# A new schedule for the attention and expert layers: fills costed at half rate first, measured durations, a new priority table

## The chip, the cores and the metric

The kernel runs on one core of one Trainium2 chip. The metric is device time in microseconds (us) of one execution. Every measured run computes the whole reference.

## The reference

Chunked attention over q, k and v of shape (4, 8, 768, 64): each chunk of 32 queries sees its own keys, 16 before, 8 after and 8 memory rows. Its output, as 3072 tokens of 512, goes through eight experts, weighted by a routing matrix that eight rounds of row and column scaling make.

```python
for c in range(nc):
    scores = scale * np.matmul(q_c, k_full.transpose(0, 1, 3, 2))
    scores = scores - np.max(scores, axis=-1, keepdims=True)
    a = np.exp(scores)
    a = a / (np.sum(a, axis=-1, keepdims=True) + 1e-09)
    out[:, :, c_start:c_end] = np.matmul(a, v_full)
...
logits = x @ w_gate
P = np.exp(logits - logits.max())
for _ in range(8):
    P /= P.sum(1, keepdims=True) + 1e-09
    P /= P.sum(0, keepdims=True) + 1e-09
    P *= N / E
for e in range(E):
    h = np.maximum(x @ w1[e], 0.0)
    ye = h @ w2[e]
    out += P[:, e:e + 1] * ye
```

## The kernel before, in words

The tokens come in 24 attention blocks of 128 queries; four blocks make a unit of 512 tokens, and there are six units. Each of the eight experts works through the six units. A product of two f32 numbers is done as three f16 products (a high and a low part of each), and the products of experts 1 to 7 go through a seven-product scheme on 2 by 2 blocks instead of eight products.

The start is what this case is about. For block n the names in the profile are these: `tq` and `tk` are TensorE (PE) transposes of q and k, `tx` that of the keys that other blocks share (`kx`), `sp` the scores, `ta` the transpose of the weights after the exponential, `xp` the product with the values (`v_pair` for blocks 0 and 1, `x_room` for some of the later ones), `gram_v` and `gram_w` PE products whose trace bounds the size of a tile, `norm_x` and `norm_w` the sums over partitions that turn such bounds into scales. `xg` is the attention output and `x` its f16 halves. `pp` is the first expert's hidden layer, `yp` its output. Later `px`, `py`, `pz` and `yx`, `yy`, `yz` do this for the other experts. `w1f` and `w2f` are the weights as they come from memory, four tiles of 512 KB each for expert 0; a tile of q or k is 256 KB, the values of one block 448 KB in pieces of up to 56 KB.

Nothing in the program text sets the order. Each step is a task with an engine, a cost in us and a priority, and `Plan.run` puts the tasks in order as if it ran them: each engine takes next the ready task of least priority value, and the instructions are issued in that order. The priority is a due time plus an entry of the table `MOVED`, by task number. In that plan a load through SyncE (SP) or GpSimd (POOL) lands after a fixed latency and a term for its bytes, at most eight are on their way at a time on either, and a task can start when those it waits for have ended. Where the plan sees PE with nothing to do for over 0.4 us, `pad` issues fills: matmuls of 256 columns whose result nobody reads (`warm` in the profile), so many that they take 0.8 of the gap at 0.11 us each. On the chip each engine runs its queue in order and waits by semaphores; a fill runs whether the gap is there or not.

The identity matrix is written by POOL; the fills read it as bf16. `v_pair` gets the eight memory rows of its batch from POOL: two small loads (`mem_v`, line 1110), and then two copies that spread them over the chunks (line 1128), which wait for the loads.

Of the kernel before, what the change touches and what calls it, by code (L numbers as in the profile page):

```python
# [120 lines left out]
class Plan:  # L121
# [73 lines left out]
    def run(self):  # L195
        clock = {e: 0.7 for e in self.ENGINES}
        waiting = {e: [] for e in self.ENGINES}
# [7 lines left out]
        while left:  # L205
# [50 lines left out]
            else:  # L256
                clock[t.eng] = t.end = at + t.cost
# [9 lines left out]
            lag = 0.0 if t.dma else 0.2 if t.eng == "PE" else 0.12  # L267
# [15 lines left out]
def tile_chunked_attn_sinkhorn_moe(  # L283
# [85 lines left out]
    idle = ident.bitcast(BF16)  # L369
# [4 lines left out]
    pscale = misc.tile([P, E, NT], F32, name="pscale")  # L374
# [273 lines left out]
    def cut(e, fp, which, st, ld, prio):  # L648
# [37 lines left out]
        for op in ops:  # L686
            sums.append(add("POOL", 0.95, tt(*op), [ld] + sums[-1:], prio - 5, [st, ws]))
# [27 lines left out]
        else:  # L715
            pieces = [(slice(2, 3), slice(0, 1), (0.5, 0.65)), (slice(4, 7), slice(1, 4), (0.9, 1.1))]
# [25 lines left out]
    def squares(total, src, deps, prio, bufs):  # L742
# [6 lines left out]
        return add("ACT", 1.2, go, deps, prio, bufs)  # L749

    def norm_scale(c, r, u, shift, name, deps, prio, slow=False):
# [24 lines left out]
        if slow:  # L776
# [12 lines left out]
            0.3,  # L789
# [14 lines left out]
    def gram(total, parts, name, deps, prio, bufs, m=P):  # L804
# [8 lines left out]
        t = add("PE", 0.5, go, deps, prio - FIRM, bufs, takes=g)  # L813
# [5 lines left out]
        return add("DVE", 0.5, trace, [t], prio, frees=g)  # L819
# [6 lines left out]
    def norm_of(fp, which, st, ld, on, prio):  # L826
# [19 lines left out]
        return c, add("DVE", 1.31, go, [ld], prio, [st])  # L846
# [38 lines left out]
    def plain1(fp, st, ld, prio):  # L885
# [9 lines left out]
                (0.6, 0.72),  # L895
# [76 lines left out]
    def load_extra(u):  # L972
# [47 lines left out]
        def part(r, loads, at, tx, takes):  # L1020
            t = add("PE", 0.6, lambda: turn(r), loads, at, [kx, kxT], takes=takes)
# [67 lines left out]
    def load_values(n):  # L1089
# [68 lines left out]
        if n < BU:  # L1158

            if n > 1:  # L1160

                vmem[slot] = b
                lv = [add("POOL", 2.0, take_m, vs[0][1], at, [vt, vs[0][0]])]
# [16 lines left out]
        else:  # L1180
            lv = []
            if BU <= n < EARLY:
                vmem[slot] = b
                lv = [add("POOL", 2.0, take_m, vs[0][1], VALUES[-1], [vt, vs[0][0]])]
# [29 lines left out]
        elif n in BY_DVE:  # L1214
# [5 lines left out]
            vfound.append(add("DVE", 1.31, most, lv, at, [vt]))  # L1220
# [11 lines left out]
    def transposed(n):  # L1232
# [35 lines left out]
        t = add("PE", 0.5, go_q, [lq], at, [qt, qT], takes=tq)  # L1268
# [1355 lines left out]
```

## Time and profile before

| | us |
|---|---|
| median of three runs | 1907.76 (1907.01 to 1907.77) |
| profiled execution | 1908.04 |
| its span, first to last instruction | 1905.9 |
| PE busy in it | 1890.7 |
| VectorE (DVE) busy | 1452.3 |
| ScalarE (ACT) busy | 1046.9 |
| POOL busy | 537.6 |

PE is busy for 99% of the span, but busy counts the 103 fills too, all in the first 50 us, and the end of a matmul is modelled: a gap of some 0.15 us behind a group does not show. What can be saved without changing the arithmetic is the time in which PE does fills or waits.

### The profile page before, as it was taken

To read this page: it belongs to the slowest core of one execution; us is meant where nothing else is said; L and a number is where in the kernel's file an instruction comes from. 1 tells how busy PE (TensorE), PEld (TensorE's weight loads), DVE (VectorE), ACT (ScalarE), POOL (GpSimd) and SP (SyncE) were. 2 spreads that over 40 slices of the span, in tenths; PEclk is the share of its full clock that TensorE was granted. 3 is DMA by queue.
4 is the path that set the end of the run, shared out by engine and by line. 5 is a ranking of instruction groups with operands and counts; after the bars stand their busy time and mean duration, and the time that the engine had idled before them with its cause. 6 is when DMAs were issued, how large, how long until landed. Compare 5 with 4: busy or idle time off the path is not lost.

```text
span 1905.9 us, 47378 instructions
## 1 busy us (share of the span) xinstructions
PE 1890.7 (99%) x19598; PEld 1629.7 (86%) x19598; DVE 1452.3 (76%) x2447; ACT 1046.9 (55%) x2047; POOL 537.6 (28%) x599
## 2 busy tenths in 40 slices
PE   8999999999999999999999999999999999999999
PEld 7677676788888888888888888888888888888888
DVE  6777669887689866888669876898678885786565
ACT  5776665655565555456456544655555563564453
POOL 3331212413134212522224131442124231332112
PEclk9999999999999999999999999999999999999999
DMA  9977744533324441364234432245313732322321
GB/s 200 206 179 219 180 156 144 174 138 112 122 87 153 167 149 46 94 230 149 84 99 164 148 128 106 89 161 184 122 46 118 247 106 103 93 84 87 125 84 67
DMA packets 207128, 254.76 MB, mean 134 GB/s; under 512 B 106112, under 2 KB 140016, under 8 KB 202560
## 3 DMA queue, kind: packets, MB, share of 16 engines
q1 hardware_dynamic: 204960, 249.63, 41.1%
q0 software_dynamic: 1952, 2.11, 0.6%
q8 instruction: 153, 2.51, 0.6%
q14 instruction: 63, 0.52, 0.1%
HBM read 187.83 MB, written 63.44 MB: 132 GB/s over the span
## 4 chain that ended last, share of the span: by engine, by line
PE 92%; DMA 3%; DVE 2%; SPq 1%; issue 1%; ACT 0%; POOL 0%; ACTq 0%; DVEq 0%; POOLq 0%
PE px L1825 25%; PE yx L1825 22%; PE pz L1825 12%; PE yz L1825 11%; PE py L1825 6%; PE yy L1825 6%; PE yp L2422 5%; PE xp L1375 1%; DMA q<-in_q_dram 1%; PE sp L1308 1%; SPq L1141 1%; DVE ss L1994 0%; DMA v_pair<-in_v_dram 0%; PE tq L1245 0%; PE ta L1365 0%
## 5 line engine op out<-in xcount | busy, mean ns | idle before, releaser
L1825 PEld LDWEIGHTS <-w 128*128 128x128 f16 x7896 | 771.4, 98 | 94.9 <-issue 4.1
L1825 PEld LDWEIGHTS <-h 128*128 128x128 f16 x7056 | 690.4, 98 | 81.5 <-issue 1.4
L1825 PE MATMUL px<-x,w 128*128 128x256 f16 x4512 | 548.5, 273 | 1.5 <-DVE c L1895 1.3
L2159 POOL TENSOR_TENSOR acc<-acc,y 128x256 f32<-128x256 f32 x252 | 263.5, 1052 | 875.5 <-ACT y L2134 862.6
L1825 PE MATMUL yx<-w,h 128*128 128x256 f16 x4032 | 468.0, 273 | 0.7 <-DVE acc L2169 0.5
L1885 ACT ACTIVATE q<-px 128x256 f32<-128x256 f32 x376 | 143.1, 382 | 286.6 <-PE px L1825 282.4
L1825 PE MATMUL pz<-x,w 128*128 128x256 f16 x2256 | 278.4, 273 | 0.0
L1825 PE MATMUL yz<-w,h 128*128 128x256 f16 x2016 | 233.8, 273 | 0.0
L2054 DVE TENSOR_TENSOR h<-ss,h 128x1024 f16<-128x1024 f32 x168 | 217.2, 1295 | 3.6 <-ACT h L2030 3.6
L2005 ACT ACTIVATE h<-c 128x768 f16<-128x768 f32 x168 | 141.0, 840 | 114.3 <-DVE c L1895 114.3
L2030 ACT CAST h<-ss 128x1024 f16<-128x1024 f32 x168 | 174.4, 1041 | 39.7 <-DVE ss L1994 39.7
L1994 DVE SCALAR_TENSOR_TENSOR ss<-c,ss 128x256 f32<-128x256 f32 x336 | 176.4, 525 | 8.5
L2038 DVE SCALAR_TENSOR_TENSOR h<-c,h 128x768 f16<-128x768 f32 x168 | 170.1, 1016 | 9.2 <-ACT h L2005 9.2
L1895 DVE SCALAR_TENSOR_TENSOR c<-px,q 128x256 f32<-128x256 f32 x188 | 77.8, 421 | 94.3 <-PE px L1825 89.0
L2134 ACT ACTIVATE y<-yx,pscale 128x256 f32<-128x256 f32 x168 | 79.8, 475 | 119.6 <-PE yx L1825 115.2
L1825 PE MATMUL py<-x,w 128*128 128x256 f16 x1128 | 139.1, 273 | 1.3 <-DVE c L1895 0.8
L2422 PE MATMUL yp<-w,h 128*128 128x512 f16 x576 | 130.9, 379 | 0.0
L1994 DVE SCALAR_TENSOR_TENSOR ss<-c,h 128x512 f32<-128x512 f32 x168 | 125.7, 748 | 1.9 <-ACT h L1982 1.9
L1895 DVE SCALAR_TENSOR_TENSOR c<-py,q 128x256 f32<-128x256 f32 x188 | 78.0, 421 | 62.0 <-PE py L1825 59.6
L1825 PE MATMUL yy<-w,h 128*128 128x256 f16 x1008 | 116.9, 273 | 0.0
L2422 PEld LDWEIGHTS <-h 128*128 128x128 f16 x576 | 55.3, 99 | 60.1 <-issue 0.2
L1895 DVE SCALAR_TENSOR_TENSOR c<-pz,q 128x256 f32<-128x256 f32 x188 | 78.2, 422 | 25.4 <-PE pz L1825 23.7
(193 smaller groups left out, 1767.2 us busy)
## 6 DMA issues: line engine op xcount, KB each, us to landing
x<-xkeep SPq DMA_DIRECT2D x28, 1792.0 KB
akeep<-acc SPq DMA_DIRECT2D x168, 256.0 KB
acc<-akeep SPq DMA_DIRECT2D x168, 256.0 KB
w1f<-in_moe_w_dram SPq DMA_DIRECT2D x36, 512.0 KB
w2f<-in_moe_w_dram SPq DMA_DIRECT2D x32, 512.0 KB
w1fm<-in_moe_w_dram SPq DMA_DIRECT2D x28, 512.0 KB
w2fm<-in_moe_w_dram SPq DMA_DIRECT2D x28, 512.0 KB
xkeep<-x SPq DMA_DIRECT2D x6, 1792.0 KB
```

Source lines behind the costliest of these rows:

```text
L1141: queue.dma_start(vt.t[p0 + r : p0 + r + m, c, :, 0:D], v[b, par::2, t : t + m].rearrange("h t d -> t h d"),)
L1825: nc.tensor.matmul(dst.t, a, b, start=(not more and n == 0), stop=(n == end), skip_group_check=more,)
L1885: lambda: nc.scalar.activation(t.t, src.t, AF.Copy, scale=down),
L1895: lambda: nc.vector.scalar_tensor_tensor(c.t[:, o], src.t, down, q.t, op0=ALU.mult, op1=ALU.add),
L1994: lambda: nc.vector.scalar_tensor_tensor(dst(), src(), 0.0, other(), op0=ALU.max, op1=op),
L2005: lambda: nc.scalar.activation(h.t[:, 0, 0:3], c.t, AF.Relu),
L2030: lambda: nc.scalar.copy(h.t[:, 0, 3:7], ss.t),
L2038: lambda: nc.vector.scalar_tensor_tensor(h.t[:, 1, 0:3].rearrange("p a n -> p (a n)"), c.t.rearrange("p a n -> p (a n)"), 0.0, h.t[:, 0, 0 ...
L2054: lambda: spare.tensor_tensor(h.t[:, 1, 3:7], ss.t, h.t[:, 0, 3:7], op=ALU.subtract),
L2134: (lambda: nc.scalar.activation(t.t, src.t, AF.Copy, scale=f))
L2159: lambda: nc.gpsimd.tensor_tensor(acc.t[:, cols], acc.t[:, cols], q.t, op=ALU.add),
L2422: nc.tensor.matmul(py.t, hf.t[:, hl, where[fh], o : o + P], room(fp, WIDE * wl + DM * fh, WIDE * wl + DM * (fh + 1)), start=(fp == 0 and i ...
```

## The change

The arithmetic and its instructions stay; the order of the instructions, the number of the fills and what they read change. Five parts:

- `pad` counts fills at 0.22 us each up to 6.9 us (`COLD`) and at 0.11 us beyond, starts no earlier than 1.1 us, and keeps the bank taken until the gap's end. PE tasks that start before 6.9 us count double.
- The fills read `pscale`, a tile that DVE clears as its first instruction; before they read the identity.
- An engine is free for the next task a little before the end of the last one (`OVER`), the latency from ACT, DVE and POOL to another engine goes from 0.12 to 0.07 us, and POOL starts at 1.6 us.
- Some thirty task costs are set to other values, PE's mostly lower, DVE's mostly higher.
- The table `MOVED` has other entries.

```diff
 MOVED = {
-    0: -85.9, 1: 16.9, 3: -259.1, 8: 9, 10: 220.9, 14: -3.9, 15: -12.2, 21: -4.5, 27: 32.3, 28:
+    3: 39.9, 8: 8.4, 11: 0.8, 14: -2.3, 27: -9, 31: 0.9, 38: -16.4, 40: -62, 43: 21, 46: 1.9,
...
+COLD = 6.9
+OPEN = 1.1
+OVER = {"ACT": 0.1, "DVE": 0.08, "POOL": 0.07}
...
+        now = max(now, OPEN)
+        cold = max(0.0, min(at, COLD) - now)
         for banks in self.free.values():
             if banks and banks[0][0] <= now + 0.2:
-                n = int((at - now - 0.1) * 0.8 / 0.11)
+                n = int(cold / 0.22) + int((at - now - cold - 0.1) * 0.8 / 0.11)
                 if n > 0:
                     _, bank = heappop(banks)
                     self.fill(bank, n)
-                    heappush(banks, (now + 0.11 * n + 0.2, bank))
+                    heappush(banks, (at, bank))
...
+        clock["POOL"] = 1.6
...
-                clock[t.eng] = t.end = at + t.cost
+                cost = 2.0 * t.cost if t.eng == "PE" and at < COLD else t.cost
+                t.end = at + cost
+                clock[t.eng] = t.end - OVER.get(t.eng, 0.0)
...
-            lag = 0.0 if t.dma else 0.2 if t.eng == "PE" else 0.12
+            lag = 0.0 if t.dma else 0.2 if t.eng == "PE" else 0.07
...
+    pscale = misc.tile([P, E, NT], F32, name="pscale")
+    nc.vector.memset(pscale, 0.0)
+    idle = pscale.rearrange("p e t -> p (e t)").bitcast(BF16)
     ident = misc.tile([P, P], F32, name="ident")
     make_identity(nc, ident)
...
-    idle = ident.bitcast(BF16)
...
-            nc.tensor.matmul(wp, idle[:, 0:P], idle, start=True, stop=True)
+            nc.tensor.matmul(wp, idle[:, 0:P], idle[:, 0:256], start=True, stop=True)
...
-        t = add("PE", 0.9, go, made + (after_v[1:2] if n == BU // 2 else []), at, [qT, kC, s], takes=sp, many=n > 1)
-        t = add("DVE", 0.7, most, [t], at, [sm], frees=sp)
+        t = add("PE", 0.8, go, made + (after_v[1:2] if n == BU // 2 else []), at, [qT, kC, s], takes=sp, many=n > 1)
+        t = add("DVE", 0.88 if blk in (0, NB - 1) else 0.69, most, [t], at, [sm], frees=sp)
```

The first place is the start of PE's queue, up to the scores of block 0. The numbers at the end of a name count tiles. Before:

```order
L482 LDWEIGHTS ident
L482 MATMUL warm<-ident 128x256
...
L790 MATMUL norm_w_3_239<-mxs,one 128x1
L1245 MATMUL tq_246<-ident,q_170 128x128 x4
L1016 MATMUL tx_254<-ident,kx_166 128x64 x4
...
L1249 MATMUL tk_268<-ident,k_174 128x128 x4
...
L1308 MATMUL sp_308<-kC,qT_259 32x64 x32
```

With the change:

```order
L494 LDWEIGHTS pscale
L494 MATMUL warm<-pscale 128x256
...
L1257 MATMUL tq_207<-ident,q_167 128x128 x4
...
L1261 MATMUL tk_218<-ident,k_169 128x128 x4
...
L1028 MATMUL tx_243<-ident,kx_172 128x64 x4
...
L1320 MATMUL sp_268<-kC,qT_213 32x64 x32
```

Before, 48 fills stand ahead of the first real matmul, 4 ahead of `tk` and 12 behind it; now 17 stand ahead of it, 2 ahead of `tk`, 11 ahead of `tx` and 9 ahead of `sp`. The scale of the weight tile `w1f_3` (`norm_w_3`) is gone from the front.

The second place is POOL's queue of loads at the start: `kx` are shared keys, the rows from `in_mem_v_dram` are the memory values, and `v_pair<-v_pair` are the copies that spread them. Before:

```order
L1000 DMA kx_166<-in_k_dram 32x8x64
L992 DMA kx_166<-in_k_dram 24x8x64
L993 DMA kx_166<-in_mem_k_dram 8x8x64
L1110 DMA v_pair<-in_mem_v_dram 8x4x64 x2
L1000 DMA kx_166<-in_k_dram 32x8x64 x2
L1128 DMA v_pair<-v_pair 8x7x260 x2
```

With the change:

```order
L1004 DMA kx_172<-in_k_dram 24x8x64
L1005 DMA kx_172<-in_mem_k_dram 8x8x64
L1012 DMA kx_172<-in_k_dram 32x8x64
L1122 DMA v_pair<-in_mem_v_dram 8x4x64 x2
L1140 DMA v_pair<-v_pair 8x7x260 x2
```

One of the two loads of shared keys that stood behind the memory values now stands ahead of them.

The third place is PE's queue from the values of block 0 (`gram_v`) to the first product of the hidden layer (`pp_0_0`). Before:

```order
L811 MATMUL gram_v_379<-v_pair 64x64
...
L1365 MATMUL ta_401<-ident,s_360 128x128 x4
...
L1375 MATMUL xp_425<-v_pair,at_413 32x65 x32
L1245 MATMUL tq_463<-ident,q_284 128x128 x4
...
L1308 MATMUL sp_498<-kC,qT_480 32x64 x32
...
L811 MATMUL gram_v_552<-v_pair 64x64
...
L1365 MATMUL ta_584<-ident,s_543 128x128 x4
L1245 MATMUL tq_589<-ident,q_461 128x128 x4
...
L2262 MATMUL pp_0_0_598<-x_532,w_0_0_423 128x128
```

With the change:

```order
L823 MATMUL gram_v_348<-v_pair 64x64
...
L1377 MATMUL ta_368<-ident,s_327 128x128 x4
L802 MATMUL norm_x_379<-vnorm,one 128x1
...
L823 MATMUL gram_w_1_386<-w1f_1_252 128x128
L1387 MATMUL xp_397<-v_pair,at_381 32x65 x32
...
L1257 MATMUL tq_459<-ident,q_301 128x128 x4
L802 MATMUL norm_w_1_469<-mxs,one 128x1
...
L1261 MATMUL tk_505<-ident,k_316 128x128 x4
...
L2274 MATMUL pp_0_0_511<-x_478,w_0_0_375 128x128
```

Scores, values' bound and weights of block 1 (`sp_498`, `gram_v_552`, `ta_584`) stood ahead of `pp_0_0` and now stand behind it; the bound of weight tile 1 (`gram_w_1`) has moved ahead of it, and 7 and 18 fills stand in the stretch between `xp` and `tk`. There are 114 fills in all, against 103, and both kernels have the same 17,843 other matmuls. From the second product of `px` of expert 0, unit 5 and weight tile 3 on, some 330 us into the run, the last 14,239 matmuls stand in the same order in both.

## Rows read from the trace of the kernel before

**Rows 1.** The page, part 1: busy time, share of the span, instructions.

```profile
PE 1890.7 (99%) x19598; PEld 1629.7 (86%) x19598; DVE 1452.3 (76%) x2447; ACT 1046.9 (55%) x2047; POOL 537.6 (28%) x599
```

**Rows 2.** The page, part 4: the chain that ended last, by engine.

```profile
PE 92%; DMA 3%; DVE 2%; SPq 1%; issue 1%; ACT 0%; POOL 0%; ACTq 0%; DVEq 0%; POOLq 0%
```

**Rows 3.** Stretches: length, busy PE, PEld, DVE, ACT, POOL, PE clock, DMA share, GB/s.

```profile
0.00:26.49 26.49, 23.09 (x367) 18.30 (x368) 13.33 (x35) 10.84 (x22) 12.88 (x25) 1.00 1.01 172
26.49:50.49 24.00, 20.90 (x506) 18.90 (x504) 17.69 (x42) 19.14 (x39) 5.06 (x9) 1.00 1.02 223
50.49:160.00 109.51, 106.19 (x1971) 75.41 (x1967) 85.31 (x157) 80.99 (x166) 39.35 (x54) 1.00 0.83 211
160.00:1890.00 1730.00, 1727.82 (x16652) 1505.92 (x16650) 1332.55 (x2207) 934.03 (x1819) 476.72 (x506) 1.00 0.38 128
1890.00:1905.93 15.93, 12.70 (x117) 11.14 (x114) 3.38 (x7) 1.90 (x4) 3.55 (x5) 0.98 0.20 67
```

**Rows 4.** The fills (tile warm) by stretch: length, busy PE (count), clock, DMA.

```profile
0.00:9.90 9.90, 8.30 (x48) 1.00 0.95 160
9.90:26.49 16.59, 5.70 (x43) 1.00 1.05 179
26.49:50.49 24.00, 1.96 (x12) 1.00 1.02 223
```

**Rows 5.** Fills that start in 1.5 to 4.0 us, and in 8.0 to 9.9 us.

```profile
L482 PE MATMUL warm<-ident x12: 392/421/421, 1.6 to 3.9; 128*128 128x256 bf16 x12
...
L482 PE MATMUL warm<-ident x18: 272/273/273, 7.7 to 9.6; 128*128 128x256 bf16 x18
```

**Rows 6.** Order of time, start, length, engine; idle time before and its releaser.

```profile
0.83 0.08 DVE L376 MEMSET vnorm<- 128x24 f32 x1
...
1.57 8.30 PE L482 MATMUL warm<-ident 128*128 128x256 bf16 x48 [1.57 <-POOL ident masks.py:199]
9.85 0.63 PE L1245 MATMUL tq<-ident,q 128*128 128x128 f32 x4
...
13.48 0.86 PE L1308 MATMUL sp<-kC,qT 64*32 64x64 f32 x64
...
16.39 0.58 PE L811 MATMUL gram_v<-v_pair 128*64 128x64 bf16 x12 [0.46 <-DMA v_pair<-v_pair]
...
17.28 0.63 PE L1365 MATMUL ta<-ident,s 128*128 128x128 f32 x4
...
18.59 0.45 PE L1375 MATMUL xp<-v_pair,at 64*32 64x65 f32 x28
19.98 0.25 PE L1375 MATMUL xp<-v_pair,at 64*32 64x65 f32 x3 [0.94 <-issue]
```

**Rows 7.** Order of time, POOL: its loads and the copies at the start.

```profile
3.20 0.58 POOL L993 DMA_DIRECT2D kx<-in_mem_k_dram  x1
3.77 1.10 POOL L1110 DMA_DIRECT2D v_pair<-in_mem_v_dram  x2
...
10.08 1.21 POOL L1128 DMA_DIRECT2D v_pair<-v_pair  x2 [4.03 <-DMA v_pair<-in_mem_v_dram]
```

**Rows 8.** Tile v_pair up to 30 us: POOL's DMAs, issue to landing.

```profile
DMA to landing us min/median/max: 5.4/5.6/5.7
```

**Rows 9.** Order of time: block 0's output, its f16 halves, and the first pp.

```profile
24.62 0.74 DVE L576 SCALAR_TENSOR_TENSOR x<-xg,sx,x 128x512 f16<-128x512 f32 x1
...
26.49 0.83 PE L2262 MATMUL pp<-x,w 128*128 128x128 f16 x12
```

**Rows 10.** Order of time, PE, up to the first yp.

```profile
43.09 0.39 PE L790 MATMUL norm_w<-mxs,one 128*128 128x4 f32 x2 [0.48 <-ACT waste L747]
44.04 0.63 PE L1249 MATMUL tk<-ident,k 128*128 128x128 f32 x4 [0.57 <-DMA k<-in_k_dram]
...
49.14 0.63 PE L1249 MATMUL tk<-ident,k 128*128 128x128 f32 x4 [1.50 <-DMA k<-in_k_dram]
49.70 0.86 PE L1375 MATMUL xp<-x_room,at 64*32 64x65 f32 x64
50.49 1.69 PE L2422 MATMUL yp<-w,h 128*128 128x512 f16 x7
```

More of the change, by code (lines that the diff above doesn't have):

```diff
@@ L373, in tile_chunked_attn_sinkhorn_moe @@
     lg = misc.tile([P, NT, E], F32, name="lg")
-    pscale = misc.tile([P, E, NT], F32, name="pscale")
     vnorm = misc.tile([P, NBLK], F32, name="vnorm")
@@ L686, in cut @@
         for op in ops:
-            sums.append(add("POOL", 0.95, tt(*op), [ld] + sums[-1:], prio - 5, [st, ws]))
+            sums.append(add("POOL", 0.8, tt(*op), [ld] + sums[-1:], prio - 5, [st, ws]))
         deps = [known[e, which], ld]
@@ L715, in cut @@
         else:
-            pieces = [(slice(2, 3), slice(0, 1), (0.5, 0.65)), (slice(4, 7), slice(1, 4), (0.9, 1.1))]
+            pieces = [(slice(2, 3), slice(0, 1), (0.53, 0.55)), (slice(4, 7), slice(1, 4), (0.95, 1.02))]
             deps = deps + o.users
@@ L747, in go @@
             nc.scalar.activation(w, a, AF.Square, accum_out=total)
-        return add("ACT", 1.2, go, deps, prio, bufs)
+        return add("ACT", 1.06, go, deps, prio, bufs)
     def norm_scale(c, r, u, shift, name, deps, prio, slow=False):
@@ L788, in norm_scale @@
             "PE",
-            0.3,
+            0.2,
             lambda: nc.tensor.matmul(total.t, ones, c, start=True, stop=True),
@@ L811, in go @@
                 nc.tensor.matmul(g.t, a, a, start=i == 0, stop=i == len(ps_) - 1)
-        t = add("PE", 0.5, go, deps, prio - FIRM, bufs, takes=g)
+        t = add("PE", 0.6, go, deps, prio - FIRM, bufs, takes=g)
         def trace():
@@ L817, in trace @@
             nc.vector.tensor_reduce(total[0:m], g.t, axis=AX.X, op=ALU.add)
-        return add("DVE", 0.5, trace, [t], prio, frees=g)
+        return add("DVE", 0.57, trace, [t], prio, frees=g)
     def halves_of(flat):
@@ L844, in go @@
             nc.vector.tensor_tensor(c, c, c, op=ALU.mult)
-        return c, add("DVE", 1.31, go, [ld], prio, [st])
+        return c, add("DVE", 1.42, go, [ld], prio, [st])
     def norms1(staged, on, prios):
@@ L894, in plain1 @@
                 prio + 0.1 * a,
-                (0.6, 0.72),
+                (0.72, 0.75),
                 [st, o],
@@ L1020, in part @@
         def part(r, loads, at, tx, takes):
-            t = add("PE", 0.6, lambda: turn(r), loads, at, [kx, kxT], takes=takes)
+            t = add("PE", 0.45, lambda: turn(r), loads, at, [kx, kxT], takes=takes)
             turns.append(t)
@@ L1162, in load_values @@
                 vmem[slot] = b
-                lv = [add("POOL", 2.0, take_m, vs[0][1], at, [vt, vs[0][0]])]
+                lv = [add("POOL", 1.06, take_m, vs[0][1], at, [vt, vs[0][0]])]
             else:
@@ L1183, in load_values @@
                 vmem[slot] = b
-                lv = [add("POOL", 2.0, take_m, vs[0][1], VALUES[-1], [vt, vs[0][0]])]
+                lv = [add("POOL", 1.06, take_m, vs[0][1], VALUES[-1], [vt, vs[0][0]])]
             lv = lv + [add(
@@ L1218, in most @@
                 nc.vector.tensor_tensor(c, c, c, op=ALU.mult)
-            vfound.append(add("DVE", 1.31, most, lv, at, [vt]))
+            vfound.append(add("DVE", 1.42, most, lv, at, [vt]))
         else:
@@ L1266, in memory @@
             nc.scalar.copy(kC.t[:, :, :, WIN:KW], src.broadcast_to([P, HP, CB, NM]))
-        t = add("PE", 0.5, go_q, [lq], at, [qt, qT], takes=tq)
+        t = add("PE", 0.45, go_q, [lq], at, [qt, qT], takes=tq)
         done = [
@@ L1279, in transposed @@
         ]
-        t = add("PE", 0.5, go_k, [lk], at, [kt, kC], takes=tk)
-        done.append(add("ACT", 0.8, windows, [t], at, [kC], frees=tk))
+        t = add("PE", 0.45, go_k, [lk], at, [kt, kC], takes=tk)
+        done.append(add("ACT", 0.72, windows, [t], at, [kC], frees=tk))
         done.append(add("ACT", 0.27, last, [t], at, [kC], frees=tk))
@@ L1346, in scores @@
         t = add(
-            "ACT", 0.6, lambda: nc.scalar.activation(s.t, s.t, AF.Exp), [t], at + 1, [s]
+            "ACT", 0.63, lambda: nc.scalar.activation(s.t, s.t, AF.Exp), [t], at + 1, [s]
         )
@@ L1381, in go @@
                         )
-        t = add("PE", 0.5, go_t, [made], at, [s, aT], takes=tp)
+        t = add("PE", 0.45, go_t, [made], at, [s, aT], takes=tp)
         t = add("ACT", 0.6, lambda: nc.scalar.copy(aT.t, tp.t), [t], at, [aT], frees=tp)
-        t = add("PE", 0.9, go, [t] + lv, at + 2, [vt, aT], takes=xp, many=n > 1)
+        t = add("PE", 0.83, go, [t] + lv, at + 2, [vt, aT], takes=xp, many=n > 1)
         after_v.append(t)
@@ L1485, in plain @@
                     at,
-                    (0.51, 0.53),
+                    (0.51, 0.75),
                     [x, g],
@@ L1500, in sums @@
             sub = ALU.subtract
-            eng, cost, spare = ("DVE", 0.6, nc.vector) if kt == 0 else ("POOL", 0.9, nc.gpsimd)
+            eng, cost, spare = ("DVE", 0.75, nc.vector) if kt == 0 else ("POOL", 0.9, nc.gpsimd)
             a = add(
@@ L1540, in sums @@
                     at,
-                    (1.15, 1.28),
+                    (1.15, 1.42),
                     [x, ts],
@@ L1558, in build @@
                         X_AT[n] + 4.0,
-                        (0.63, 0.75),
+                        (0.72, 0.75),
                         [x, g1],
@@ L1577, in build @@
                         START + 13.0,
-                        (0.63, 0.75),
+                        (0.72, 0.75),
                         bufs,
@@ L1594, in rest @@
                             at,
-                            (0.63, 0.75),
+                            (0.72, 0.75),
                             [x, g1],
@@ L1635, in logits @@
             "PE",
-            1.2,
+            1.02,
             go,
@@ L1645, in logits @@
             "PE",
-            0.3,
+            0.15,
             lambda: nc.tensor.transpose(lq.t.rearrange("p t e -> p (t e)"), lt.t[:, 0], ident),
```

47 rows, old and new, of the table MOVED are left out of this document.

## Prediction

> **What bounds the kernel now.** I read the busy times first. TensorE (PE) is busy for 1890.7 of 1905.9 us [rows 1], and the chain that ended last is PE for 92% [rows 2], so the time is PE's real work, plus the fills, plus PE's waits. The real work is the same 17,843 matmuls in both kernels, so only fills and waits can move. The stretches [rows 3] say where the waits are; length less PE's busy time is 3.4 us up to 26.49, 3.1 up to 50.49, 3.3 up to 160, then 2.2 in 1730 us, and 3.2 at the end, where PE is done and the last outputs leave. The fills [rows 4] are 48 before 9.9 us, 43 up to 26.49 and 12 up to 50.49, none later. How long one takes is read from starts, since the duration of a matmul includes a tail beside the next one [rows 5]: 11 steps between 1.6 and 3.9 us are 0.21 us each, 17 steps between 7.7 and 9.6 us are 0.11. These are the lower and the upper level of PE's clock (1.2 and 2.4 GHz), although the clock column of rows 3 shows 1.00 throughout. The 48 fills run from 1.57 to about 9.7 us [rows 6], 8.1 us. If x of them go at 0.21 and the rest at 0.11, x is 28 or 29, and the clock rises at about 7.5 us. The 55 later fills at 0.11 cost 6.0. That makes 14.1 us of fills and 12.0 of waits before the end stretch. Those 26 us are what the change plays for. They are in the start, since beyond 160 us hardly anything is left.
>
> **The change, step by step.** I follow five points of PE's queue.
>
> *Scores of block 0 (`sp`).* Before, the first real work starts when the 48 fills are through, and `sp` stands at 13.48 us [rows 6]. Now the first fill waits for DVE's clearing instead of POOL's identity. DVE clears 24 columns in 0.08 us at 0.83 [rows 6]; for 192 columns, some 0.1 to 0.25 us from 0.8, I take 1.05 as the first fill's start instead of 1.57. Seventeen fills at 0.21 end at 4.65. The four transposes of `tq`, 0.63 us with the tail at the upper level [rows 6] and some 0.45 without it, cost 0.9 at the lower, two fills 0.4, `tk` 0.9, and 11 fills (two at the lower level) 1.4: 8.25. Then `tx` waits for the memory keys, issued at 3.20 [rows 7]; POOL's loads land 5.4 to 5.7 us after issue [rows 8], so 8.8. With 0.25 for `tx` and nine fills, 1.0, `sp` starts at about 10.0, which is 3.5 us earlier.
>
> *Values of block 0 (`gram_v`).* The second part of `gram_v` reads what POOL's two copies write, and PE waited for just that at 16.39 [rows 6]. POOL had issued the memory values at 3.77 and then stood idle for 4.03 us until 10.08, when they landed [rows 7]. Now a load of shared keys of some 0.6 us stands ahead of them, so they land at about 10.7, the copies go out until 11.9, and with the 5.1 us from the last copy's issue to PE's start that rows 7 and 6 show (11.29 to 16.39) `gram_v` goes on at 17.0. PE arrives there at about 13.3 (`sp` 0.8, the second `tx` not before its keys at 11.25, `gram_w`, five fills, and the bound's trace on DVE), so it waits 3.7 us where it waited under one. What stands behind it in PE's queue is `ta`, which has nothing to do with the values and would have been ready at 13.8 (it follows `sp` by 3.8 us in rows 6). It starts at 17.5 against 17.28: the head start is gone.
>
> By the Trainium skill, "DMA: Bandwidth & Descriptors", section "Anatomy of one DMA — SWDGE (gpsimd) path", such a transfer costs about 2.0 us plus its bytes. By that the copies would have landed by 11 us, the wait of 3.7 us would not be there, and the sum below would be up to 3.5 us lower. Rows 8 show 5.4 to 5.7 for this queue at this time, so I go by them.
>
> *First product of the hidden layer (`pp_0_0`).* Before, `xp` starts at 18.59, has a hole of 0.94 us in it [rows 6], DVE ends the f16 halves of block 0 at 25.36, and `pp` starts at 26.49 [rows 9]. Now `gram_w_1` stands between `ta` and `xp`, so `xp` starts at about 18.6 as before. The halves follow by the 6.8 us of before less the hole, at 24.4, since two more scales and a half of a weight tile stand ahead of them on DVE where the second block's scores stood. The 18 fills end at 23.4 and hide behind that. `pp_0_0` starts at 24.5, 2.0 earlier. But `sp`, `gram_v`, `ta` and `tq` of block 1, 2.3 us with their small ones, are still to do, and `gram_w_1` with two sums, 0.7, is done. Net gain 0.4 us.
>
> *First output of expert 0 (`yp`).* Before it starts at 50.49 [rows 10]; with the values of block 3, which now stand ahead of it, the same work would end at 51.3. From `pp_0_0` on, before spends 24.0 us, of which 1.3 are 12 fills and 3.1 waits [rows 3, 4]; 19.6 are work. Now 19.6, plus 1.6, plus 0.85, plus 40 fills at 0.11, 4.4, give 24.5 + 26.45 = 50.95 with no wait. Loads set the other bound: PE waited for k at 44.04 and 49.14 [rows 10]. Up to the second of these, SP had loaded 8224 KB by the tiles' sizes; up to the same k of block 4 it now loads 8448, one half of a block's values more, so at the same rate k lands at 50.5. With `tk`, `ta`, six fills and `xp`, 2.4 us, that is 52.9. I take 52.2, between the two and nearer the row with the wait, 0.9 us later than before.
>
> *The rest.* Up to 160 us five more fills, 0.55. The 3.3 us of waits there [rows 3] were for late loads and for DVE; PE comes 0.9 us later, so I take 2.0, a gain of 1.3; the bounds are 0.5 and 5. Beyond some 330 us PE's order is the same, and the 2.2 us of waits (DVE behind by half a us) may go or come again: 0, with 1 us to either side. The end stretch is the same.
>
> Where costs, latencies and `OVER` only steer the order, they cost nothing by themselves. Sum against the profiled execution: 0.9 + 0.55 - 1.3 = +0.15, 1908.04 to 1908.2. The median of the runs is 0.28 below that execution, so 1907.9.
>
> **Rivals.** *The plan is right and PE hardly waits (faster).* For it: a plan with measured durations has fewer waits that it doesn't see, and 114 fills cost little more than 103 (21 at 0.21 and 93 at 0.11, 14.6 us, against 14.1). Against it: the latency of POOL's loads is not among the edits. If loads don't bind before `yp`, it starts at 50.95 less half the wait at `gram_v`, 49.1, or 2.2 earlier; with 0.5 us of waits up to 160 us (-2.8), the five fills and one of the late waits gone (-1.0), this gives -5.4, 1902.5.
>
> *POOL's transfers take 2 us (the rule above).* The gain at `gram_v` stays as far as the loads for `yp` let it: 1904.4 at best.
>
> *The weight tile that was first is late (slower).* `w1f_3` was SP's first load and is now the 43rd. `norm_w_3` on PE waits for it and for 1.4 us of DVE; behind it in PE's queue stand `tq` of block 3, the last `pp` of weight tile 2, the scores of block 3 and all `pp` of tile 3. By bytes (6944 KB to its end, against 7488 for SP's first 42, which had landed at 44.04 [rows 10]) it lands at 40.8; PE comes to it at about 42. From a landing after 40.6 on each us costs one. If it lands as late as the 42nd did, PE waits 3.4 us; the loads behind it, needed before `yp`, are as late, and `yp` starts at 55, so 1911.9 with the rest as above.
>
> *PE's clock falls in the long wait at `gram_v`.* The longest wait before, 1.50 us, was followed by a `tk` of the usual 0.63 [rows 10]; 3.7 us is not in the trace. A second rise like the first, from 1.57 to 7.5, would cost half of 5.9 us, 2.9: 1910.8. The Trainium skill, "TensorE: Matmul & The Clock Gate", section "HAM oscillation — how this bites in real kernels", describes such waits for DMAs that send the clock back; no row here shows one.
>
> *The new fills don't do what fills are for.* If zeros held the clock at the lower level, everything up to the hidden layer would go at half rate, some 8 us: 1916. The identity read as bf16 has one value in 256 that isn't zero, and rows 5 show the rise with it, so hardly.
>
> **How the numbers follow.** Forecast as summed 0.49, the plan is right 0.22, the rule 0.05, the late tile 0.16, the clock 0.05, the fills 0.03. The likeliest is 1907.9, with 1904.5 to 1911.5 as its own range. Bounds of the unknown terms (the wait at `gram_v` 0 to 4.5, loads before `yp` -1.3 to +3, waits to 160 us 0.5 to 5, late waits 1 to either side) and the cases on both sides give 1902.3 to 1912.8. 0.2%, 3.8 us, is about what a measurement can tell from no change: faster takes most of the second case and little of the first, 0.21; slower half of the late tile, the fills and the forecast's upper end, 0.22; the same 0.57.
>
> **What would show it.** In the new trace: 17 fills from 1.05, `sp` near 10.0, a wait of 3 to 4 us at `gram_v` for POOL's copies, `pp` near 24.5, waits for k, w1f or w2f between 40 and 51, the first `yp` near 52, then under 3 us of waits up to 160. The forecast is wrong if `gram_v` doesn't wait, if `yp` starts before 50 or after 54, or if the stretch beyond 330 us differs by over 1.5 us.

## The result and the profile after

The changed kernel takes 1932.45 us (median of 4 runs, 1931.79 to 1936.49), the kernel before 1907.76 beside it (1907.01 to 1910.5): ratio 1.0131, 95% interval 1.0114 to 1.0149. That is 24.7 us slower; the forecast was 1907.9 with a range up to 1912.8. The profiled execution spans 1931.1 us, 25.2 more than the one of before.

From the page of after, the busy times and the shares of the chain that ended last, which answer to [rows 1, 2]:

```profile
PE 1895.1 (98%) x19609; PEld 1633.0 (85%) x19609; DVE 1426.3 (74%) x2448; ACT 1020.8 (53%) x2047; POOL 539.3 (28%) x599
...
PE 81%; DVE 6%; issue 5%; POOL 4%; DMA 2%; ACT 2%; SPq 0%; POOLq 0%; DVEq 0%; ACTq 0%
```

PE is busy for 4.4 us more and idle for 20.8 more; the chain, PE's for 92% before, now goes over DVE and POOL as well. The stretches of both kernels tell where. They are cut where PE has done the same work: at the end of expert 0's last output, at the start of expert 1's first output group (`yx`, unit 5), and at the end of that group. Columns as in [rows 3]. After:

```profile
0.00:369.69 369.69, 359.24 (x5582) 259.45 (x5582) 269.68 (x558) 232.88 (x464) 107.93 (x146) 0.99 0.67 179
369.69:388.03 18.34, 18.34 (x170) 16.44 (x168) 15.46 (x27) 12.98 (x27) 6.03 (x8) 1.00 0.78 269
388.03:420.51 32.48, 20.69 (x170) 17.58 (x168) 17.37 (x29) 11.60 (x22) 7.79 (x8) 0.79 0.28 82
420.51:1931.10 1510.59, 1496.82 (x13694) 1339.54 (x13691) 1123.81 (x1836) 763.31 (x1536) 417.50 (x439) 1.00 0.36 120
```

Before, at the same points of the work:

```profile
0.00:367.47 367.47, 357.64 (x5571) 257.29 (x5572) 272.53 (x556) 233.53 (x464) 102.85 (x146) 1.00 0.69 177
367.47:385.81 18.34, 18.34 (x170) 16.44 (x169) 16.01 (x25) 12.62 (x26) 7.25 (x8) 1.00 0.80 287
385.81:404.15 18.34, 18.34 (x171) 16.45 (x169) 16.45 (x24) 7.11 (x15) 5.19 (x6) 1.00 0.25 76
404.15:1905.90 1501.75, 1496.37 (x13694) 1339.51 (x13691) 1147.27 (x1844) 793.64 (x1544) 422.27 (x440) 1.00 0.36 122
```

The differences of the lengths are 2.2, 0, 14.1 and 8.8 us, together the 25.2. So the first stretch, with the start that the prediction was mostly about, has 2.2 of it. The loss lies where PE's order is the same in both kernels, and 14.1 us lie in one stretch of seven products of 24 matmuls. The waits of PE beyond 160 us, after and before, with the total, the count and the longest:

```profile
PE yx L1837 <- DVE acc L2181: 16.1, 6, 11.8
PE pz L1837 <- ACT q L1897: 7.1, 6, 1.3
PE cp L1773 <- DVE cs L1745: 1.2, 3, 0.6
...
```

```profile
PE px L1825 <- DVE c L1895: 1.3, 2, 0.9
PE yx L1825 <- DVE acc L2169: 0.5, 1, 0.5
```

One wait of 11.8 us, and some of about a microsecond that come again with each expert: from 420 us on 5.8 us for `q` and 4.3 for `acc`, 10.1 in all, against 1.8 before. Those 8.3 are nearly all of the last stretch's 8.8. In the first stretch the changed kernel waits 2.3 us between 327 and 349 us: two waits for `cs`, 1.0, and one for `q`, 1.3; the groups of matmuls that they cut in two add some 0.5 by their tails. At the first `px` of expert 1, just ahead of these waits (327.28, before 328.40), it is 1.1 us ahead, or 0.6 if the two `cp` are counted that it still has to do.

**The one long wait.** In order of time, the rows of PE, POOL, ACT and DVE of the changed kernel around it (start, length, engine, idle time before and its releaser):

```profile
396.82 3.65 POOL L2171 TENSOR_TENSOR acc<-acc,y 128x256 f32<-128x256 f32 x2 [4.13 <-ACT y L2146]
398.14 0.15 DVE L512 TENSOR_REDUCE most_of<-mxs 128x2 f32<-128x8 f32 x1
...
398.77 0.47 ACT L2146 ACTIVATE y<-yz,pscale 128x256 f32<-128x256 f32 x1 [0.23 <-PE yz L1837]
401.13 2.78 PE L1837 MATMUL yz<-w,h 128*128 128x256 f16 x24
...
406.35 0.37 POOL L536 PARTITION_ALL_REDUCE most_of<-most_of  x1 [5.87 <-issue]
406.75 0.17 DVE L517 TENSOR_SCALAR most_of<-most_of 128x2 f32<-128x2 f32 x1 [2.24 <-POOL most_of L536]
...
414.42 1.40 POOL L2171 TENSOR_TENSOR acc<-acc,y 128x256 f32<-128x256 f32 x2 [7.70 <-ACT w L580]
415.16 0.48 DVE L2181 SCALAR_TENSOR_TENSOR acc<-yx,pscale,acc 128x256 f32<-128x256 f32 x1 [7.44 <-POOL acc L2171]
415.70 4.97 PE L1837 MATMUL yx<-w,h 128*128 128x256 f16 x24 [11.79 <-DVE acc L2181]
```

POOL adds the two halves `y6`, then reduces the weight scale of expert 2 over the partitions (`most_of`), then adds the two halves `y5`. The last `y5` is there at 399.24, but the adds start at 414.42. The reduce itself is a row of 0.37 us; POOL does nothing else from 400.47 to 414.42, 14.0 us, of which 5.87 lie ahead of the row and 7.70 behind it. The releaser named for the 7.70, ACT's split of a weight, has nothing to do with `y5`: it is only the last event before the start. DVE's `acc` follows the first add and PE's `yx` follows that. Then `yx` takes 4.97 instead of 2.78 us, 2.2 more. The granted clock of the stretch is 0.79: 1.00 up to 405 us, 0.50 from 407 to 420. POOL's queue at this place, before on the left and after on the right (numbers of `y` left out):

```
L2159 acc_1_22<-acc_1_22,y6    L2171 acc_1_22<-acc_1_22,y6
L2159 acc_1_23<-acc_1_23,y6    L2171 acc_1_23<-acc_1_23,y6
L2159 acc_1_20<-acc_1_20,y5    L536  most_of<-most_of
L2159 acc_1_21<-acc_1_21,y5    L2171 acc_1_20<-acc_1_20,y5
L524  most_of<-most_of         L2171 acc_1_21<-acc_1_21,y5
```

**The start.** PE's rows that answer to those of [rows 6, 9, 10]:

```profile
1.11 3.33 PE L494 MATMUL warm<-pscale 128*128 128x256 bf16 x17 [1.11 <-DVE pscale L376]
4.27 0.60 PE L1257 MATMUL tq<-ident,q 128*128 128x128 f32 x4
...
6.41 0.63 PE L1261 MATMUL tk<-ident,k 128*128 128x128 f32 x4 [1.32 <-DMA k<-in_k_dram]
...
9.65 0.86 PE L1320 MATMUL sp<-kC,qT 64*32 64x64 f32 x64
...
11.92 0.63 PE L823 MATMUL gram_w<-w1f 128*128 128x128 bf16 x8 [1.02 <-DMA w1f<-in_moe_w_dram]
...
15.06 0.85 PE L823 MATMUL gram_v<-v_pair 128*64 128x64 bf16 x12 [1.05 <-DMA v_pair<-v_pair]
15.84 1.12 PE L1377 MATMUL ta<-ident,s 128*128 128x128 f32 x4
...
23.99 1.81 PE L2274 MATMUL pp<-x,w 128*128 128x128 f16 x24
...
53.85 2.33 PE L2434 MATMUL yp<-w,h 128*128 128x512 f16 x10
```

And by stretches, as in [rows 3]; the granted clock is the third number from the end. Up to 10 us it shows 1.00, although the first 12 fills, up to 3.5 us, take 0.21 us each, the time of the lower level. The mean of 0.90 from 10 to 15 us means one microsecond at half: it fell at 14.0, behind the first wait of a microsecond (up to 11.92) and just as the second (up to 15.06) began. By the 0.91 from 20 to 25 it was back at 20.9.

```profile
10.00:15.00 5.00, 2.71 (x71) 2.04 (x54) 2.62 (x8) 1.90 (x4) 3.39 (x6) 0.90 1.10 239
15.00:20.00 5.00, 4.94 (x95) 4.26 (x96) 3.62 (x11) 1.86 (x4) 4.05 (x4) 0.50 1.19 247
20.00:25.00 5.00, 4.85 (x47) 4.12 (x46) 4.46 (x15) 3.94 (x8) 0.00 (x0) 0.91 0.83 162
```

### The profile page after: what moved, and what is told of

It is laid out like the page before. It is cut to its first block, busy times and chain, and to the rows that moved or that the text cites. A ratio compares the mean times of both kernels' runs of the same rounds, so it can differ in the third digit from the quotient of the medians.

```text
span 1931.1 us, 47357 instructions
## 1 busy us (share of the span) xinstructions
PE 1895.1 (98%) x19609; PEld 1633.0 (85%) x19609; DVE 1426.3 (74%) x2448; ACT 1020.8 (53%) x2047; POOL 539.3 (28%) x599
## 4 chain that ended last, share of the span: by engine, by line
PE 81%; DVE 6%; issue 5%; POOL 4%; DMA 2%; ACT 2%; SPq 0%; POOLq 0%; DVEq 0%; ACTq 0%
PE px L1837 21%; PE yx L1837 20%; PE pz L1837 10%; PE yz L1837 9%; PE yp L2434 5%; PE py L1837 5%; PE yy L1837 5%; POOL ws L668 2%; DVE ss L2006 2%; DVE w L588 2%; POOL acc L2171 1%; PE xp L1387 1%; PE sp L1320 1%; DMA acc<-akeep 1%; ACT w L580 1%
## 5 line engine op out<-in xcount | busy, mean ns | idle before, releaser
L2171 POOL TENSOR_TENSOR acc<-acc,y 128x256 f32<-128x256 f32 x252 | 267.4, 1070 | 946.2 <-ACT y L2146 922.5
L2050 DVE SCALAR_TENSOR_TENSOR h<-c,h 128x768 f16<-128x768 f32 x168 | 165.7, 1004 | 9.0 <-ACT h L2017 9.0
L2006 DVE SCALAR_TENSOR_TENSOR ss<-c,ss 128x256 f32<-128x256 f32 x336 | 168.3, 536 | 0.0
L580 ACT ACTIVATE w<-ws,sw 128x1024 f16<-128x1024 f32 x56 | 64.1, 1145 | 96.8 <-POOL ws L668 96.7
```

Of the source, the lines that this page charges most:

```text
L580: lambda: nc.scalar.activation(dst(0), src(), AF.Copy, scale=s),
L2006: lambda: nc.vector.scalar_tensor_tensor(dst(), src(), 0.0, other(), op0=ALU.max, op1=op),
L2050: lambda: nc.vector.scalar_tensor_tensor(h.t[:, 1, 0:3].rearrange("p a n -> p (a n)"), c.t.rearrange("p a n -> p (a n)"), 0.0, h.t[:, 0, 0 ...
L2171: lambda: nc.gpsimd.tensor_tensor(acc.t[:, cols], acc.t[:, cols], q.t, op=ALU.add),
```

## The experiments

Ratios are to the kernel before on the same chip, with their 95% interval. PE's order is the changed kernel's in all but the second and the eighth experiment, where it is that of before, and the tenth, which adds 38 fills. Experiments 3 and 4 leave out a part of the work or of the data and so do not compute the reference; they serve to find the cause.

**1. The reduce behind the adds.** A time before which the plan may not start the reduce (task 1588); beyond 455 us nothing moves.

```diff
+        if t.n in (1588,):
+            t.ready = 391.0
```

> The changed kernel, with GpSimd's reduce for the weight scale of expert 2 placed two places later on GpSimd's queue, behind the two adds of y5 (PE's order is word for word the same). Theory A: PE's wait of 11.8 us at 403.91 is GpSimd being held from 400.47 to 414.42, 14.0 us, by that reduce, and the 2.2 us that the next yx takes longer is the clock that fell in the wait. Then both go: 1932.4 - 14.0 = 1918.4, 1917 to 1920, and the waits of about 1 us once per expert stay (8 us together). Rival B: the adds wait for their accumulators, whose loads and ACT scales end at 408 to 410, or for DVE's late work. Then the wait stays within 3 us of its length, 1929 to 1933.

Measured 1918.96 us, 1.0057 (1.0042 to 1.0072): 13.5 less than the changed kernel. The long wait is gone; the waits for `q` (7.2 us) and `acc` (3.4) are still there. Theory A holds, B falls.

**2. The same order in the kernel before.** The two adds (tasks 1662, 1665) may not start before 403.3 us, so that the reduce comes first.

```diff
+        if t.n in (1662, 1665):
+            t.ready = 403.3
```

> The kernel before, with the two y5 adds put behind the reduce on GpSimd's queue (PE's order the same). DVE hands the reduce its input at 402.49, PE comes to the yx that needs the adds at 401.53. Theory A: the 14 us hold now stands between them: GpSimd is free again at about 412 to 414, PE waits 11 to 14 us and the next yx takes 2.2 us longer: 1907.8 + 13 to 16 = 1921 to 1924. Rival B (the adds have slack, the reduce is not what holds them): 1907 to 1910.

Measured 1919.51 us, 1.0061 (1.0046 to 1.0076), 12.3 more than before and 1.5 under the range of theory A; rival B falls. PE's row of this run, and then POOL's:

```profile
410.18 4.71 PE L1827 MATMUL yx<-w,h 128*128 128x256 f16 x24 [10.74 <-DVE acc L2171]
```

```profile
400.58 0.37 POOL L526 PARTITION_ALL_REDUCE most_of<-most_of  x1 [6.75 <-DVE most_of L502]
408.89 1.40 POOL L2161 TENSOR_TENSOR acc<-acc,y 128x256 f32<-128x256 f32 x2 [7.94 <-ACT acc L2087]
```

The swap alone makes the wait, in the old kernel too, and the slow `yx` behind it (4.71 us instead of 2.78).

**3. GpSimd without its sums.** As the first run; the weights' sums are not computed.

```diff
+            if e > 0:
+                return lambda: eng.memset(ws.t[:, i], 1.0)
```

> As the first run, and for experts 1 to 7 GpSimd's 4 sums per weight tile are left out: a memset of the same place stands for each, in the same order, so the weights' sums are not computed. Theory C: the waits of about 1 us that come back once per expert (pz for ACT's q, yx for DVE's acc; 8.3 us from 420 on) come from DVE, whose two-input operations take 0.95, 1.21 and 1.48 us where they take 0.41, 0.68 and 0.95 alone, whenever GpSimd works on two-input operations of its own; without GpSimd's sums DVE's chain is on time and the waits go: 1918.4 - 7 = 1911, 1909.5 to 1913, with DVE's busy time lower by tens of us. Rival D: the waits come from the order of ACT's queue (the cast of ss ahead of q), whatever DVE's speed: 1917 to 1920.

Measured 1903.44 us, 0.9977 (0.9967 to 0.9987), 6 us below the range of theory C. No wait of PE beyond 160 us is left, where the first run has 12.9 us of them; the medians differ by 15.5, twice the 7 expected, since it is not only the waits that come once per expert that go. Below is the same unit in the first run and in this one, in order of time; first run, DVE, POOL, ACT and PE:

```profile
604.24 1.38 POOL L670 TENSOR_TENSOR ws<-w1f 128x256 f32<-128x256 f32 x1 [2.58 <-DVE w L590]
604.95 1.22 DVE L2008 SCALAR_TENSOR_TENSOR ss<-c,h 128x512 f32<-128x512 f32 x1
...
606.97 1.48 DVE L2052 SCALAR_TENSOR_TENSOR h<-c,h 128x768 f16<-128x768 f32 x1
607.59 1.44 POOL L670 TENSOR_TENSOR ws<-w1f,ws 128x256 f32<-128x256 f32 x1
608.37 0.94 DVE L2008 SCALAR_TENSOR_TENSOR ss<-c,ss 128x256 f32<-128x256 f32 x1
...
609.34 1.05 ACT L2044 CAST h<-ss 128x1024 f16<-128x1024 f32 x1 [1.99 <-DVE ss L2008]
610.29 0.65 ACT L1899 ACTIVATE q<-pz 128x256 f32<-128x256 f32 x2
610.72 1.47 PE L1839 MATMUL pz<-x,w 128*128 128x256 f16 x12 [1.17 <-ACT q L1899]
```

This run, another expert's turn of the same unit, DVE and ACT:

```profile
816.28 0.69 DVE L2010 SCALAR_TENSOR_TENSOR ss<-c,h 128x512 f32<-128x512 f32 x1
...
817.61 0.96 DVE L2054 SCALAR_TENSOR_TENSOR h<-c,h 128x768 f16<-128x768 f32 x1
818.48 0.42 DVE L2010 SCALAR_TENSOR_TENSOR ss<-c,ss 128x256 f32<-128x256 f32 x1
819.06 1.04 ACT L2046 CAST h<-ss 128x1024 f16<-128x1024 f32 x1
819.99 0.66 ACT L1901 ACTIVATE q<-pz 128x256 f32<-128x256 f32 x2
```

Beside POOL's sums three operations of DVE take 0.53, 0.52 and 0.52 us more. ACT's cast of `ss` waits 1.99 us for them, ACT's `q` stands behind the cast, and PE's `pz` waits for `q`. ACT's order is the same in both, so of rival D the words "whatever DVE's speed" fall. Its order does not. The kernel before has the same slow operations at the same cast, and `pz` doesn't wait; DVE, ACT and PE of before:

```profile
602.87 1.48 DVE L2038 SCALAR_TENSOR_TENSOR h<-c,h 128x768 f16<-128x768 f32 x1
604.26 0.94 DVE L1994 SCALAR_TENSOR_TENSOR ss<-c,ss 128x256 f32<-128x256 f32 x1
...
603.06 0.38 ACT L1885 ACTIVATE q<-pz 128x256 f32<-128x256 f32 x1 [0.27 <-PE pz L1825]
605.24 1.05 ACT L2030 CAST h<-ss 128x1024 f16<-128x1024 f32 x1 [1.80 <-DVE ss L1994]
...
604.17 1.47 PE L1825 MATMUL pz<-x,w 128*128 128x256 f16 x12
```

There the cast waits 1.80 us for `ss` too, but both `q` stand ahead of it on ACT's queue. Beyond 330 us, the traces have a cast of `ss` directly ahead of the `q` of a `pz` once in the kernel before, 40 times in the changed kernel, 39 times in experiments 1, 3 and 4, and 0 to 9 times in the others. DVE's slow operations are not new: the `ss` of 256 columns takes 525 ns in the mean before and 536 after. What the change brought is the place of the cast, and the wait of `pz` needs both. The waits of `yx` for `acc` were not followed in this way.

For the slow operations the Trainium skill has a rule, in "SBUF — State Buffer", section "SBUF: two separate sides": an operation of DVE with two inputs in SBUF and one of GpSimd that reads SBUF exclude each other, so that one of them stands still; a memset reads nothing. The rows agree; whether an operation stands still or runs slower they do not show.

**4. The splits don't wait for the sums.** As the first run, every engine's order the same; ACT's and DVE's last split of a weight tile reads the loaded tile, so the split is not that of the sums.

```diff
+                    (lambda: st.t.rearrange("p a k f -> p (a k f)" if which == 1 else "p a d -> p (a d)"))
+                    if e > 0
+                    else (lambda of=of: ws.t[:, of].rearrange(flat)),
```

> As the run with the reduce behind the adds (every engine's order word for word the same), but for experts 1 to 7 ACT's and DVE's last split of each weight tile reads the loaded tile and not GpSimd's sums (the sums are made and not used), so no split waits for them any more; ACT waited 96.7 us for them in all. Theory C (DVE slowed by GpSimd's two-input operations beside its own): the once-per-expert waits stay, 1917 to 1920, and DVE's mean of the 256-column ss stays near 533 ns. Rival I: the waits come from the splits that stand in ACT's and DVE's queues until the sums are made; then they go, 1919.0 - 8 = 1911, 1909.5 to 1913.

Measured 1919.97 us, 1.0066 (1.0050 to 1.0081). By the total rival I falls, but the waits moved, and `ss` did not stay near 533 ns: its mean is 508, against 531 in the first run. The stretch that takes 18.3 us in both kernels takes 24.3 here (371.00 to 395.26), and from there on the profile is 4.0 us behind that of before, where the first run's is 7.6. So the late sums have a share of the recurring waits that this run doesn't separate.

**5. The allowance for overlap up to 330 us only.**

```diff
-                clock[t.eng] = t.end - OVER.get(t.eng, 0.0)
+                clock[t.eng] = t.end - (OVER.get(t.eng, 0.0) if at < 330.0 else 0.0)
```

> The changed kernel, with the plan's allowance for overlap (OVER: 0.1, 0.08, 0.07 us off each operation of ACT, DVE, GpSimd) only up to 330 us of the plan. PE's order is the same; ACT's, DVE's and GpSimd's differ in hundreds of places, and the reduce stands behind the y5 adds. Theory E: the allowance is what leaves DVE without room, and without it both the hold of 14 us and the recurring waits go: 1909 to 1912. Rival F: only the hold goes, the recurring waits come from something else (GpSimd's sums being counted shorter, or the table): 1917 to 1920.

Measured 1910.88 us, 1.0020 (1.0010 to 1.0029), as theory E has it. The reduce comes behind the adds without the edit of the first run, and `pz` and `yx` wait for nothing.

**6 and 7. Whose allowance it is.** Both with the edit of the first run; DVE's alone ends at 330 us, and then those of ACT and POOL alone.

```diff
+                clock[t.eng] = t.end - (OVER.get(t.eng, 0.0) if at < 330.0 or t.eng != "DVE" else 0.0)
+                clock[t.eng] = t.end - (OVER.get(t.eng, 0.0) if at < 330.0 or t.eng == "DVE" else 0.0)
```

> As the run with the reduce behind the adds, with DVE's allowance (0.08 us off each operation) only up to 330 us; those of ACT and GpSimd stay. PE's order is the same. Theory E': it is DVE that the plan takes for faster than it is, so this alone takes away the recurring waits: 1910 to 1912.5. Rival J: it takes all three, or ACT's 0.1: 1915 to 1920.

> The counterpart: the reduce behind the adds, ACT's and GpSimd's allowance only up to 330 us, DVE's stays. Theory E': the recurring waits stay, 1916 to 1920. Rival J: they go, 1910 to 1913.

Measured 1911.12 us, 1.0019 (1.0010 to 1.0028), and 1916.53 us, 1.0049 (1.0032 to 1.0066), both within the ranges of theory E'. Without DVE's 0.08 us per operation 7.8 of the 8.1 us between the first run and the fifth are gone. Without the other two allowances 2.4 us are gone, which the intervals of these runs don't tell from none; there the waits of `pz` for `q` fall from 7.2 to 1.2 us, and waits for `c` (3.5) and `acc` (1.9) stay.

**8. DVE's allowance in the kernel before.**

```diff
-                clock[t.eng] = t.end = at + t.cost
+                t.end = at + t.cost
+                clock[t.eng] = t.end - (0.08 if t.eng == "DVE" and at > 330.0 else 0.0)
```

> The kernel before, whose plan now takes 0.08 us off each operation of DVE beyond 330 us, and nothing else; table, costs, fills and start are those of before, PE's order is the same and the reduce still stands behind the y5 adds. Theory E': this one line brings the recurring waits with it: 1907.8 + 5 to 8 = 1913 to 1916, with PE waiting once per expert for ACT's q or DVE's acc. Rival K: the waits belong to the new table or to the lower cost of GpSimd's sums: 1907 to 1909.5.

Measured 1909.86 us, 1.0013 (1.0003 to 1.0022): 2.4 us slower, where theory E' asked for 5 to 8 and rival K for 1.7 at most; neither range has it. PE waits 2.1 us for `acc` and 2.0 for `c`. So the allowance alone does not bring the 8 us. Which of the new plan's other constants it needs beside it, no run shows.

**9. The changed start, the old late part.** Beyond 330 us no allowance, 0.12 us of latency and 0.95 for a sum.

```diff
-            lag = 0.0 if t.dma else 0.2 if t.eng == "PE" else 0.07
+            lag = 0.0 if t.dma else 0.2 if t.eng == "PE" else 0.07 if at < 330.0 else 0.12
-            sums.append(add("POOL", 0.8, tt(*op), [ld] + sums[-1:], prio - 5, [st, ws]))
+            sums.append(add("POOL", 0.8 if e < 2 else 0.95, tt(*op), [ld] + sums[-1:], prio - 5, [st, ws]))
```

> The changed kernel up to 330 us of the plan, and beyond it the plan's old constants (no allowance, 0.12 us of latency, 0.95 us for a sum of GpSimd). PE's order is that of the changed kernel. What it is off the kernel before is what the new start is worth. Theory L (the start's terms cancel, as the forecast summed them): 1907 to 1909. Theory M (the clock, which fell between 15 and 25 us in every profile of the new start, makes the start dearer): 1909.5 to 1912.

Measured 1908.94 us, 1.0006 (0.9998 to 1.0015). Theory L holds in the total, at the edge of its range, and the interval, up to 1910.3 us, reaches into that of theory M: with the late part's constants back, the new table, costs and fills of the start cannot be told from those of before. It is not the clean "start alone": up to expert 0's last output this profile is 2.2 us behind that of before, and 1.2 ahead from there on.

**10. Fills in the two waits of the start.** On top of the fifth run.

```diff
+EXTRA = {("w1_0", 0): 14, ("v_0", 4): 24}
+                if (name, i) in EXTRA:
+                    z = idle[:, 0:m]
+                    for j in range(EXTRA[name, i]):
+                        nc.tensor.matmul(g.t, z, z, start=i + j == 0, stop=False)
```

> As the run with the allowance up to 330 us, with 14 fills of 128 columns put in front of block 0's gram_w and 24 fills of 64 columns (zeros added to the sum) between its fourth and fifth gram_v product, the two places where PE waited 1.24 and 1.06 us in that run and after which the granted clock fell to 0.66 from 15 to 20 us (0.90, 0.50, 0.91 from 10 to 25 in the profile of the changed kernel). Theory G: those waits cost the clock, 1.5 to 3 us, and fills in them keep it at 1.00 at almost no cost: 1910.9 - 1.5 = 1909.4, 1907.5 to 1910. Rival H: PE's share of work between 10 and 20 us stays too low whatever stands in these two waits, or such fills don't count: the clock falls as before, 1910.5 to 1912.

Measured 1911.8 us, 1.0028 (1.0017 to 1.0039), no faster than the fifth run. The stretches:

```profile
10.00:15.00 5.00, 4.61 (x126) 3.85 (x125) 2.61 (x8) 1.47 (x4) 3.56 (x7) 1.00 1.03 224
15.00:20.00 5.00, 3.70 (x104) 3.02 (x100) 2.77 (x7) 1.73 (x3) 3.54 (x4) 1.00 1.20 263
20.00:25.00 5.00, 3.10 (x18) 2.46 (x16) 3.68 (x15) 2.46 (x5) 0.51 (x1) 0.73 0.65 142
```

The fills keep the clock at 1.00 up to 20 us. But PE still waits 1.25 us ahead of the fifth `gram_v` product, for copies that land later in this profile (it goes on at 16.44, in the fifth run's at 15.55), and 1.90 us for ACT ahead of `norm_w` (0.65 there), and from 20 to 25 us the clock is 0.73. The profiled execution also has one hole of 4.12 us at 40.61 that no other profile has, so its size is not read. Theory G is right on the clock up to 20 us and wrong on the time.

The medians put in a row (their runs of before lie between 1907.2 and 1907.8) give where the 24.7 us are (25.0 against the last of these): the reduce ahead of the adds 13.5 (1932.45 to 1918.96), DVE's allowance 7.8 (to 1911.12), those of ACT and POOL 0.2 (to 1910.88), latency and cost of the sums 1.9 (to 1908.94), the start 1.5 (to 1907.43). The last is no measurable difference, and the intervals on both sides of the 1.9 overlap. The steps hold for this order of taking things away, as experiments 6 and 7 show. Only the run without the sums is faster than the kernel before.

## Why the prediction was wrong

- **The step that failed** is the last sentence of "The rest": "Beyond some 330 us PE's order is the same, and the 2.2 us of waits ... may go or come again: 0, with 1 us to either side." It measured +23: 14.1 and 8.8, with 1.3 more for `q` just ahead of them. PE's order was the same, but what PE waits for is set by the other engines' order there, and that I did not read. On POOL's queue the reduce now stands two places earlier, and on ACT's the cast of `ss` stands ahead of `q`. The sentence "Where costs, latencies and `OVER` only steer the order, they cost nothing by themselves" covered it up: they steered it on three engines over 1570 us.
- **It could be seen beforehand.** Where no task is ready, the plan takes on each engine the one that can start first, whatever its priority. Written out as the changed kernel is built, its own times say that the reduce can start at 389.19 and the `y5` adds at 389.49 and 390.58; it counts 14.0 us for the reduce and then has PE wait 9.67 us. So 0.3 us of a plan decided, and the plan knew of the loss. In the plan of before, the adds can start at 395.98 and 397.09 and the reduce at 403.17, well behind them. What the plan of the changed kernel doesn't know are the recurring waits: it shows none, because DVE, which has hardly any idle time in this unit, is counted 0.08 us faster per operation and as if POOL's sums didn't slow it.
- **The size "1 us to either side"** came from before, where DVE was behind three times, by 0.4 to 0.9 us. That shows how little room DVE had, not that there was some.
- **Scores of block 0**: first fill at 1.11 (1.05), `tq` at 4.27 (fills to 4.65), `sp` at 9.65 (10.0). Right, in part by luck: the last four or five of the 17 fills took 0.11 us instead of 0.21, and PE waited 1.32 us for k ahead of `tk`, neither of which the forecast had.
- **Values of block 0**: `gram_v` goes on at 15.06 (17.0) after 1.05 us (3.7). The landing times of [rows 8] were too long for the memory values: they landed 4.3 us after issue here, the copies 5.3. By the Trainium skill, "DMA: Bandwidth & Descriptors", section "Anatomy of one DMA — SWDGE (gpsimd) path", it would be about 2.0 us and the bytes; these rows show over twice that, so the rival that rests on it falls too.
- **The clock** fell, the rival with a chance of 0.05, at 14.0 us, behind a wait of 1.02 us and at the beginning of one of 1.05 rather than in one of 3.7; that put back most of what `gram_v` won, `ta` taking 1.12 us instead of 0.63. The Trainium skill, "TensorE: Matmul & The Clock Gate", section "HAM oscillation — how this bites in real kernels", describes such falls in waits for DMAs of some 3 to 5 us. These rows have the fall, but beside waits of 1.02 and 1.05 us.
- **`pp` and `yp`**: `pp` at 23.99 (24.5), right; `yp` at 53.85 (52.2): from 25 us on 1.9 us of waits, none of them put down to a load, and from `pp` on some 1.5 us more work than I had summed.
- **Up to 160 us**: no wait from 53.85 on, where I took 2.0. With that the start's sum is near zero, as forecast, by other terms: 0.6 us ahead by the profile at 327 us, 1.5 behind by the medians of experiment 9, within the noise.
- **Late weight tile, dead fills**: neither happened. No wait for `w1f_3` is there, and the zeros brought the clock up by 4.3 us. The late tile's 1911.9 was also added up wrong: `yp` at 55 instead of 52.2 makes 1907.9 + 2.8 = 1910.7.
- **What would make the prediction wrong** named the right place: the stretch beyond 330 us differs by over 1.5 us.

## What to carry to other kernels

When one engine's order is the same in both kernels, compare the queues of those that it waits for, and look first for the one long instruction on them: a greedy planner starts it whenever it is ready a little earlier than short work that the critical engine needs. Then look for an instruction that waits ahead of one that the critical engine needs, as ACT's cast stands ahead of `q`. Slack in a plan's costs can carry what the plan doesn't know: 0.08 us off each operation of DVE was worth 7.8 us in the changed kernel and 2.4 in the kernel before. So take margins off only for engines that are not nearly full, and not where another engine's work slows them.

## What the hardware showed that was not expected

- A reduce over the partitions on GpSimd holds it 14 us for a row of 0.37: 5.87 and 7.70 us of idle time around it in the changed kernel, 6.75 and 7.94 in experiment 2. DVE has the result 7.7 us before GpSimd goes on. The plan of both kernels counts 14.0 us for it. In the program as built, a reload of GpSimd's library stands ahead of each reduce, and another ahead of GpSimd's next arithmetic instruction; the two idle stretches lie at these places, but no run takes the reloads away. In the kernel before, DMA issues stand between the first reduce and the second reload, and the first two of them go out at once, at 209.42, beside the end of the reduce's row (209.17 to 209.54). The Trainium skill, "GPSIMD Engine Reference", section "2.1 Instruction dispatch", gives some 6 us for the first call of code that was just loaded; the part ahead of the row, 5.87 and 6.75 us, is of that size.
- The same start differs from execution to execution by more than the change of the start is worth: the 48 fills of before took 8.30 us in the profile that I argued from, and 6.86 and 7.06 in experiments 2 and 8, where expert 0's last output then ended 2.3 us earlier.
- A wait of 10.7 to 11.8 us of PE costs some 2 us more in the next product (4.71 and 4.97 us against 2.78), and nothing after that: the `px` behind it takes its usual 1.47 us in both runs.
